# Splitting the first chunk's second-layer weights between the steps of the first projection, and taking weight tiles at the split

## The chip, the core and the metric

The kernel runs on one core of one Trainium2 chip. Its metric is the device time of one execution in microseconds (us). Five engines take part: TensorE (PE, with its weight loads shown apart as PEld), VectorE (DVE), ScalarE (ACT), GpSimd (POOL) and SyncE (SP), which here issues the DMAs.

## What is computed

A transformer block with adaptive layer norm, in fp32: S = 2048 rows, D = 576, H = 32 heads of 18, a hidden layer of 4608.

```python
mod = (silu(c) @ w_mod).reshape(1, 6, 1, 576)          # sa, ca, ga, sb, cb, gb
h = layernorm(x) * (1 + ca) + sa
x = x + ga * (softmax(q @ k.T * Dh**-0.5) @ v  @ wo)    # q, k, v = h @ wqkv, 32 heads
h = layernorm(x) * (1 + cb) + sb
x = x + gb * (silu(h @ w1) @ w2)
```

## The kernel before

**Blocks and slots.** The 2048 rows are taken as four blocks of 512. For each block the attention runs head quad by head quad (8 quads), and its inner work is cut into slots: per slot TensorE makes two score matmuls into `psa` (line 812; VectorE takes their maximum, `mx`, line 814) and two into `psb` (line 863; ScalarE takes their exponential into `pt`, line 865). The products with V go to `psv` (line 900). All the other matmul work of the preceding block is laid between the slots as "filler": the output projection (`psp`, function `proj`), the second layer norm, the transposes of its result (`psT`, `h_T`), and the two layers of the MLP (`ps1`, `mlp1`; `ps2`, `mlp2`).

**Who sets the order.** TensorE's order is written out by the code: a planner (`Plan`) keeps an estimated time `plan.t`, and at each turn a slot, a piece of PV or a piece of filler is put down. Data decides when an instruction may start, but TensorE never runs a later instruction ahead of an earlier one. The loop also calls `serve` once a turn, which puts down the handling of weights described next. VectorE, ScalarE, POOL and SP have each one queue in program order as the framework's scheduler has put it.

**Precision and weights.** Every matmul is done in fp32r with operands in a high and a low part, so a weight tile has two halves in its second dimension. In block 0 the weights come raw from the inputs: `load_half` issues a DMA of half a tile into one of three `raw` buffers; `split_half` makes the parts on POOL. A half of `wo` or of `w2` takes three POOL instructions (multiply by the gate `ga` or `gb`, line 701; cast to the high part, line 702; subtract for the low part, line 705), a half of `w1` two (lines 704 and 705). `split_half` is put down when its load is `LAND` planner-ns old; its first instruction waits for the last score matmul put down ahead of it (`after_pe`). After the second half, `store_one` writes the split tile to a scratch array, `STORE` planner-ns later. Blocks 1 to 3 read the split tiles from there. `settle` puts down whatever is missing when a matmul needs the tile.

**MLP in chunks.** 36 tiles of `w1` and of `w2` are used in chunks of four (`CH`): `mlp1` for four hidden tiles (in pairs), then `mlp2` for the four 128-row tiles j of the block. `w1` tiles live in a ring of four (`W1B`), `w2` tiles in a ring of five; `wo` uses the same two rings before them.

**The stage around the change**, in block 0: `o_T` splits the attention output into `th` and `tl`; then the projection runs for j = 0 to 3, 14 parts each. At its end `add_x1` adds it to the residual `x1`: one half of the columns on VectorE (line 1010), the other through ScalarE (`gt`, line 1013) and POOL (line 1014). The layer norm of tile j follows while the projection of tile j + 1 runs: statistics (`ln_stat`, line 1020, two instructions, the second needs POOL's half of the add; aggregate, line 1023), the power on POOL (`r`, line 388), four small VectorE instructions (`ln_rs`, lines 394 to 398), the normalised row (`ob`, line 402) and a 64-column copy on POOL (line 403). Then eight planner-us without filler (`LP`), five `h_T` (transposes on TensorE, `etmp` on ScalarE, cast `hh` on VectorE, line 409, `hl` on POOL, line 413; the last one with `h2`, line 1053, and 64 rows of `hh`, line 415, both on POOL), and the first `mlp1`. In between are the loads of `w1` tiles 0 to 3 and `w2` tiles 0 to 3; `w1` tiles 4 and 5 are asked for while the second `mlp1` runs.

## Time and profile before

| | us |
|---|---|
| three timed runs | 2376.93, 2377.96, 2383.35 |
| their median | 2377.96 |
| the profiled execution's own time | 2377.5 |
| its span, first to last instruction | 2375.7 |
| PE busy | 2306.1 |
| DVE busy | 1784.3 |
| ACT busy | 1479.9 |
| POOL busy | 714.1 |

The times named below count from the start of the span. The output projection of block 0 runs from 567 to 598 us, its five `h_T` from 608 to 616, its MLP from 616 to about 1146. The profile's pages show for each engine the busy time, for each group of instructions what ended the idle time before it, and in slices the clock that was granted to TensorE (1.00 is full, 0.50 half). Matmul ends are modelled, so that a matmul row that follows another closely says little about how full TensorE is; an idle gap with the name of an instruction that ended it says more.

### The profile page before, as it was taken

What the parts mean: (1) busy time and instruction counts of PE and PEld (TensorE: products, weight loads), DVE (VectorE), ACT (ScalarE), POOL (GpSimd) and SP (SyncE); (2) the same over time, 40 slices, a digit from 0 to 9 for tenths busy, and PEclk for the clock granted to TensorE, in tenths of its full rate; (3) what the DMA queues carried; (4) which work ended last, traced back from release to release, by engine and by line L of the source; (5) the groups of instructions that cost most, each with busy time, mean ns of one, the idle gap of its engine ahead of it and who ended that gap; (6) DMA issues with size and microseconds to landing.
All of it is one profiled execution on the core that took longest, in us unless ns stands there. A gap on an engine that the chain in (4) does not pass through costs nothing.

```text
span 2375.7 us, 52168 instructions
## 1 busy us (share of the span) xinstructions
PE 2306.1 (97%) x19844; PEld 1576.7 (66%) x19844; DVE 1784.3 (75%) x3089; ACT 1479.9 (62%) x2710; POOL 714.1 (30%) x873
## 2 busy tenths in 40 slices
PE   5999999998899999999999999999999999989999
PEld 4874444434467777766666766767676676678998
DVE  8768889887878888887888888887888887144333
ACT  5237777775667777775777777775777777722121
POOL 5113433315747676654211111122211111110000
PEclk9999999999999999999999999999999999999999
DMA  7455556454656666665654445554655554335663
GB/s 254 161 178 173 177 169 183 161 173 152 210 183 223 216 226 219 220 214 172 220 183 168 158 164 192 168 183 134 201 160 188 177 187 153 114 134 208 214 204 115
DMA packets 201475, 433.02 MB, mean 182 GB/s; under 512 B 31362, under 2 KB 67618, under 8 KB 201226
## 3 DMA queue, kind: packets, MB, share of 16 engines
q1 hardware_dynamic: 201226, 429.68, 54.9%
q8 instruction: 159, 2.61, 0.5%
q14 instruction: 90, 0.74, 0.1%
HBM read 338.54 MB, written 86.33 MB: 179 GB/s over the span
## 4 chain that ended last, share of the span: by engine, by line
PE 85%; DVE 6%; DMA 3%; POOL 2%; ACT 2%; issue 1%; SPq 0%; DVEq 0%; POOLq 0%; ACTq 0%
PE ps L486 25%; PE psv L900 18%; PE psa L812 14%; PE ps L480 10%; PE psb L863 8%; PE psqk L599 4%; DVE mx L814 2%; PE psv L486 2%; PE psp L486 1%; DMA raw<-in_w 1%; PE psqk L486 1%; PE psv L1361 1%; ACT pt L865 1%; PE psqk L1361 1%; PE psp L480 1%
## 5 line engine op out<-in xcount | busy, mean ns | idle before, releaser
L814 DVE TENSOR_REDUCE mx<-psa 128x1 f32<-128x512 f32 x2048 | 1329.9, 684 | 285.3 <-PE psb L863 153.6
L865 ACT ACTIVATE pt<-psb 128x512 f32<-128x512 f32 x2048 | 1143.0, 598 | 482.6 <-PE psb L863 294.0
L863 PE MATMUL psb<-qt,kb 56*128 56x512 f32 x2048 | 754.6, 422 | 7.9 <-ACT pt L865 7.4
L812 PE MATMUL psa<-ka,qt 54*128 54x512 f32 x2016 | 722.8, 416 | 9.2 <-DVE mx L814 8.0
L812 PEld LDWEIGHTS psa<-ka,qt 54*128 54x128 f32 x2016 | 339.7, 186 | 306.3 <-DVE mx L814 204.6
L900 PE MATMUL psv<-pt,vt 128*32 128x512 f32 x4096 | 512.0, 603 | 1.0 <-ACT ov L904 1.0
L486 PE MATMUL ps<-w2t,g 64*128 64x288 f32 x4992 | 408.6, 293 | 0.9 <-POOL w2t L705 0.6
L486 PEld LDWEIGHTS ps<-w2t,g 64*128 64x128 f32 x4992 | 382.8, 186 | 29.1 <-DVE mx L814 5.0
L863 PEld LDWEIGHTS psb<-qt,kb 56*128 56x128 f32 x2048 | 352.6, 185 | 48.5 <-ACT pt L865 32.9
L486 PE MATMUL ps<-hh,w1t 64*128 64x512 f32 x1944 | 359.9, 395 | 5.2 <-POOL w1t L704 1.8
L1136 POOL TENSOR_TENSOR g<-etmp,g 128x512 fp32r<-128x512 f32 x108 | 137.6, 1295 | 381.4 <-ACT g L1135 269.7
L900 PEld LDWEIGHTS psv<-pt,vt 128*32 128x32 f32 x4096 | 100.0, 109 | 211.6 <-issue 205.1
L486 PEld LDWEIGHTS ps<-hh,w1t 64*128 64x128 f32 x1944 | 197.8, 187 | 50.6 <-DVE mx L814 5.9
L1014 POOL TENSOR_TENSOR x<-x,gt 128x288 f32<-128x288 f32 x116 | 93.1, 803 | 424.6 <-ACT gt L1013 424.6
L486 PE MATMUL ps<-hl,w1t 64*128 64x512 f32 x864 | 180.9, 393 | 0.0
L1010 DVE TENSOR_TENSOR x<-ps,x 128x288 f32<-128x288 f32 x184 | 83.9, 456 | 127.0 <-PE ps L480 76.5
L480 PE MATMUL ps<-w2t,g 128*128 128x288 f32 x960 | 132.9, 299 | 7.4 <-ACT g L1135 5.9
L480 PEld LDWEIGHTS ps<-w2t,g 128*128 128x128 f32 x960 | 130.5, 191 | 9.9 <-ACT g L1135 6.3
L1132 ACT ACTIVATE eq<-ps 128x512 f32<-128x512 f32 x36 | 21.5, 598 | 146.4 <-PE ps L480 146.4
L480 PE MATMUL ps<-hh,w1t 128*128 128x512 f32 x360 | 106.9, 390 | 0.5 <-DVE hh L415 0.5
L486 PEld LDWEIGHTS ps<-hl,w1t 64*128 64x128 f32 x864 | 90.2, 187 | 15.3
L1133 DVE SCALAR_TENSOR_TENSOR etmp<-etmp 128x512 f32<-128x512 f32 x108 | 78.5, 765 | 23.6 <-ACT etmp L1132 22.9
(150 smaller groups left out, 2138.4 us busy)
## 6 DMA issues: line engine op xcount, KB each, us to landing
w1t<-w1s SPq DMA_DIRECT2D x108, 640.0 KB
w2t<-w2s SPq DMA_DIRECT2D x108, 576.0 KB
kb<-kscr SPq DMA_DIRECT2D x512, 108.0 KB
ka<-kscr SPq DMA_DIRECT2D x504, 108.0 KB
w1s<-w1t SPq DMA_DIRECT2D x36, 640.0 KB
w2s<-w2t SPq DMA_DIRECT2D x36, 576.0 KB
vt<-vscr SPq DMA_DIRECT2D x32, 608.0 KB
qt<-qscr SPq DMA_DIRECT2D x128, 108.0 KB
```

The costliest lines, as they stand in the source:

```text
L480: mm(self.ps[late], lhsT=lhsT, rhs=rhs, start=(i == 0), stop=(i == self.n - 1))
L486: done = mm(self.ps[g], lhsT=lhsT[rows], rhs=rhs[rows], start=(s == 0), stop=(s == self.end))
L599: mm(qk_ps[0], lhsT=w[b][:, kt, :], rhs=(hTl if a else hTh)[:, kt, n * 512:(n + 1) * 512], start=(i == 0), stop=(i == 13))
L812: mm(ps, lhsT=t["q"][64 * j:64 * j + 54, hp, stt * P:(stt + 1) * P], rhs=t["a" if ("a", kc, hp) in t else "b", kc, hp][64 * j:64 * j + 54, ...
L814: return lambda: nc.vector.tensor_reduce(t["mx"][:, 2 * j + hp, stt, kc:kc + 1], ps, axis=AX.X, op=ALU.max)
L863: state["pe"] = mm(ps, lhsT=t["b", kt // 4, hp][64 * e:64 * e + 56, kt % 4 * P:(kt % 4 + 1) * P], rhs=t["q"][64 * e:64 * e + 56, hp, :], s ...
L865: nc.scalar.activation(t["P"][kt, hp][:, e, :], ps, AF.Exp, scale=SCALE)
L900: mm(t["ps"][32 * h:32 * h + 32, :], lhsT=t["v"][:, c0:c0 + 32], rhs=t["P"][kt, h // 2][:, h % 2, :], start=(kt == 0), stop=(kt == NKT - 1 ...
L1010: nc.vector.tensor_add(c["x1"][j][:, hs], ps, c["x1"][j][:, hs])
L1014: nc.gpsimd.tensor_add(c["x1"][j][:, hs], c["x1"][j][:, hs], t)
L1133: nc.vector.scalar_tensor_tensor(t, t, 1.0, u, op0=ALU.add, op1=ALU.mult)
L1136: (nc.vector if last else nc.gpsimd).tensor_tensor(g[:, 1, :], t, f(g[:, 0, :]), op=ALU.subtract)
```

## The change

Four things change, all of them in block 0 but for the two numbers.

- `w2` tiles 0 to 3 are asked for at parts 1, 4, 7 and 10 of the first projection (j = 0), not after the last norm step. `w1` tiles 2 and 3 are asked for after the fourth and fifth `h_T`, tiles 4 and 5 at parts 9 and 11 of the first `mlp1`. For the last chunk the last three `w2` tiles are asked for near the end of the preceding `mlp2`.
- A flag `ln` keeps `serve` from putting down a split from the end of a tile's projection to that tile's `ln_rs`.
- A tile of the ring is taken when its first half is split (`make`), not when it is asked for; `hold` keeps the split back until the ring's old tile has been used, and a store of the old tile that is still due is put down first.
- `LAND` goes from 5000 to 6000 planner-ns, `STORE` from 4000 to 8000.

The instructions of TensorE, VectorE and ScalarE are the same ones in the same order as before. POOL has the same instructions in another order, and so has SP with its DMAs.

**Place 1.** POOL's queue behind the first projection of block 0. `x` is the residual of a tile (its number tells tiles apart), `r` the power of the norm, `ob` the normalised row. Before:

```order
L1014 TENSOR_TENSOR x_6608<-x_6608,gt 128x288
L388 TENSOR_TENSOR r_7272<-ve,mhalf 128x1
L403 COPY ob<-ob 128x64
L1014 TENSOR_TENSOR x_6610<-x_6610,gt 128x288
L388 TENSOR_TENSOR r_7385<-ve,mhalf 128x1
L403 COPY ob<-ob 128x64
```

Of the change (lines 707, 708 and 711 are 701, 702 and 705 of before, 1023 is 1014):

```order
L1023 TENSOR_TENSOR x_6603<-x_6603,gt 128x288
L388 TENSOR_TENSOR r_7278<-ve,mhalf 128x1
L403 COPY ob<-ob 128x64
L707 TENSOR_TENSOR raw<-raw,gb 128x288 x2
L708 CAST w2t<-raw 128x288 x2
L711 TENSOR_TENSOR w2t<-raw,w2t 128x288 x2
L1023 TENSOR_TENSOR x_6605<-x_6605,gt 128x288
L388 TENSOR_TENSOR r_7402<-ve,mhalf 128x1
```

Both halves of `w2` tile 0 now stand between the copy of the first tile's `ob` and the add of the second tile's `x`. The same six stand ahead of the third tile's add (for `w2` tile 1) and of the fourth's (tile 2); of tile 3 the first half stands around the fourth tile's `r`, the second behind its `ob`.

**Place 2.** POOL's queue at the five `h_T`. `hl`, `h` (that is `h2`) and `hh` are what the first `mlp1` reads. Before:

```order
L704 CAST w1t<-raw 128x320
L413 TENSOR_TENSOR hl<-etmp,hh 128x512
L705 TENSOR_TENSOR w1t<-raw,w1t 128x320
L413 TENSOR_TENSOR hl<-etmp,hh 128x512
L704 CAST w1t<-raw 128x320
L705 TENSOR_TENSOR w1t<-raw,w1t 128x320
L704 CAST w1t<-raw 128x320
L413 TENSOR_TENSOR hl<-etmp,hh 128x512
L701 TENSOR_TENSOR raw<-raw,gb 128x288
L705 TENSOR_TENSOR w1t<-raw,w1t 128x320
L1053 CAST h_7841<-etmp 128x512
L415 TENSOR_TENSOR hh<-etmp,hh 64x512
```

Of the change:

```order
L710 CAST w1t<-raw 128x320
L711 TENSOR_TENSOR w1t<-raw,w1t 128x320
L413 TENSOR_TENSOR hl<-etmp,hh 128x512 x4
L1063 CAST h_7864<-etmp 128x512
L415 TENSOR_TENSOR hh<-etmp,hh 64x512
L710 CAST w1t<-raw 128x320
L711 TENSOR_TENSOR w1t<-raw,w1t 128x320
```

No split stands any more between the `hl` and ahead of `h` and `hh`; those of `w1` tiles 2 and 3 follow them.

**Place 3.** POOL's queue ahead of `w1` tiles 4 and 5, which the third `mlp1` reads; `g` is the output of an `mlp1`. Before:

```order
L705 TENSOR_TENSOR w2t<-raw,w2t 128x288
L701 TENSOR_TENSOR raw<-raw,gb 128x288
L1136 TENSOR_TENSOR g<-etmp,g 128x512
L702 CAST w2t<-raw 128x288
L1136 TENSOR_TENSOR g<-etmp,g 128x512
L705 TENSOR_TENSOR w2t<-raw,w2t 128x288
L704 CAST w1t<-raw 128x320
L705 TENSOR_TENSOR w1t<-raw,w1t 128x320
L704 CAST w1t<-raw 128x320
L705 TENSOR_TENSOR w1t<-raw,w1t 128x320
L704 CAST w1t<-raw 128x320 x2
L705 TENSOR_TENSOR w1t<-raw,w1t 128x320 x2
```

Of the change:

```order
L710 CAST w1t<-raw 128x320
L711 TENSOR_TENSOR w1t<-raw,w1t 128x320
L710 CAST w1t<-raw 128x320
L1157 TENSOR_TENSOR g<-etmp,g 128x512
L711 TENSOR_TENSOR w1t<-raw,w1t 128x320
L1157 TENSOR_TENSOR g<-etmp,g 128x512
L710 CAST w1t<-raw 128x320
L711 TENSOR_TENSOR w1t<-raw,w1t 128x320
L710 CAST w1t<-raw 128x320
L711 TENSOR_TENSOR w1t<-raw,w1t 128x320
L710 CAST w1t<-raw 128x320
L711 TENSOR_TENSOR w1t<-raw,w1t 128x320
L1157 TENSOR_TENSOR g<-etmp,g 128x512 x2
```

Before, the halves of `w1` tiles 4 and 5 stood behind 24 instructions for `w2` tiles 0 to 3 and behind the first two `g`; now they stand around these two, and no `w2` is left ahead of them.

```diff
@@ -59,7 +59,7 @@
 LP = 8000
 PB = 9
 PVMAX, PVMIN = 5, 3
-EACH, LAND, STORE = (1500, 2000), 5000, 4000
+EACH, LAND, STORE = (1500, 2000), 6000, 8000
 QKB = 3
 GS = 2
 GR = [[range(i, min(i + GS, n)) for i in range(0, n, GS)] for n in (28, 27)]
@@ -632,7 +632,7 @@
         qk_store(which, m, n, hl, (1, 0))
 
 
-    state = {"now": 0, "pe": None, "p": 0, "b": 0, "tail": False, "tail2": False}
+    state = {"now": 0, "pe": None, "p": 0, "b": 0, "tail": False, "tail2": False, "ln": False}
     fill = Filler(plan)
     qk_w = {}
 
@@ -667,14 +667,15 @@
                         fill.add(200, lambda a=mt_: mod_piece(*a), mode="full")
 
     asks, flight, stores = [], [], []
+    RING = {"w1": W1B, "w2": 5}
     last_load = [0]
 
-    def weights(key, w, src, scr, first, gate=None):
+    def weights(key, make, n, src, scr, first, gate=None, hold=None):
 
         if not first:
-            nc.sync.dma_start(f(w), f(scr))
+            nc.sync.dma_start(f(make()), f(scr))
             return
-        ask = {"key": key, "w": w, "src": src, "scr": scr, "gate": gate, "n": w.shape[2] // 2, "at": 0, "halves": [0, 1]}
+        ask = {"key": key, "make": make, "src": src, "scr": scr, "gate": gate, "n": n // 2, "hold": hold, "halves": [0, 1]}
         i = len(asks)
         while key[0] == "w1" and i and asks[i - 1]["key"][0] == "w2" and len(asks[i - 1]["halves"]) == 2:
             i -= 1
@@ -694,6 +695,11 @@
     def split_half():
 
         _, ask, h, raw = flight.pop(0)
+        if h == 0:
+            tag = ask["key"][0] if ask["key"][0] != "wo" else None
+            while tag and any(it[3] == (tag, ask["key"][1] - RING[tag]) for it in stores):
+                store_one()
+            ask["w"] = ask["make"]()
         w, gate, n = ask["w"], ask["gate"], ask["n"]
         cs = slice(h * n, h * n + n)
         hi = w[:, 1, cs]
@@ -704,18 +710,18 @@
             after_pe(nc.gpsimd.tensor_copy(hi, raw))
         nc.gpsimd.tensor_tensor(w[:, 0, cs], raw, f(hi), op=ALU.subtract)
         if h:
-            stores.append((plan.t + STORE, w, ask["scr"]))
+            stores.append((plan.t + STORE, w, ask["scr"], ask["key"]))
 
     def store_one():
 
-        _, w, scr = stores.pop(0)
+        _, w, scr, _ = stores.pop(0)
         nc.sync.dma_start(f(scr), f(w))
 
     def serve():
 
         if stores and stores[0][0] <= plan.t:
             store_one()
-        if flight and flight[0][0] + LAND <= plan.t:
+        if flight and flight[0][0] + LAND <= plan.t and not state["ln"] and not (flight[0][1]["hold"] and flight[0][1]["hold"]()):
             split_half()
         if asks and len(flight) < 3 and last_load[0] + EACH[asks[0]["gate"] is not None] <= plan.t:
             load_half()
@@ -951,12 +957,14 @@
         pool = mp["p"]
         c = ready[b] = {}
         for kt in range(KT):
-            if kt < 4:
-                w = pool.tile([P, 2, KT * P], F32R, tag="w1", name="wo1", bufs=W1B)[:, :, :D]
-            else:
-                w = pool.tile([P, 2, D], F32R, tag="w2", name="wo2", bufs=5)
-            weights(("wo", kt), w, wo[:, kt, :], wos[kt], b == 0, ga)
-            c["wo", kt] = w
+            def make(kt=kt):
+                if kt < 4:
+                    c["wo", kt] = pool.tile([P, 2, KT * P], F32R, tag="w1", name="wo1", bufs=W1B)[:, :, :D]
+                else:
+                    c["wo", kt] = pool.tile([P, 2, D], F32R, tag="w2", name="wo2", bufs=5)
+                return c["wo", kt]
+
+            weights(("wo", kt), make, D, wo[:, kt, :], wos[kt], b == 0, ga)
         c["x1"] = []
         for j in range(NST):
             c["x1"].append(pool.tile([P, D], F32, name="x1", bufs=5))
@@ -1000,6 +1008,7 @@
             for s in GP[part]:
                 c["pp"].step(s)
             if part == len(GP) - 1:
+                state["ln"] = b == 0
                 for g in range(2):
                     add_x1(j, g, c["pp"].ps[g])
                     plan.op("AV"[g == 0], plan.t + 200, 440, c["pp"].release[g])
@@ -1026,6 +1035,7 @@
 
         def ln_rs(j):
             c["rs", j] = rstd_b(pool, *c["ve", j], 1)
+            state["ln"] = False
             plan.op("V", plan.t, 770)
 
         def ln_c(j):
@@ -1071,6 +1081,8 @@
             steps_ = dict(zip((1, 4, 8, 11), ln_steps(j - 1))) if j else {}
             for part in range(len(GP)):
                 fl.add(MMH * len(GP[part]), lambda j=j, part=part: proj(j, part), need={0: pair_need if j else o_need, len(GP) // 2: half_need}.get(part))
+                if b == 0 and j == 0 and part in (1, 4, 7, 10):
+                    fl.add(0, lambda i=part // 3: w2_load(i))
                 if part in steps_:
                     fl.add(0, steps_[part])
         for step in ln_steps(3):
@@ -1083,12 +1095,20 @@
             fl.add(LP)
 
         def w_load(i):
-            c["w1", i] = pool.tile([P, 2, KT * P], F32R, tag="w1", name="w1t", bufs=W1B)
-            weights(("w1", i), c["w1", i], w1[i], w1s[i], b == 0)
+            def make():
+                c["w1", i] = pool.tile([P, 2, KT * P], F32R, tag="w1", name="w1t", bufs=W1B)
+                return c["w1", i]
+
+            weights(("w1", i), make, KT * P, w1[i], w1s[i], b == 0, None, lambda: i >= c["room"])
 
         def w2_load(i):
-            c["w2", i] = pool.tile([P, 2, D], F32R, tag="w2", name="w2t", bufs=5)
-            weights(("w2", i), c["w2", i], w2[i], w2s[i], b == 0, gb)
+            def make():
+                c["w2", i] = pool.tile([P, 2, D], F32R, tag="w2", name="w2t", bufs=5)
+                return c["w2", i]
+
+            weights(("w2", i), make, D, w2[i], w2s[i], b == 0, gb, lambda: i > c["freed"] + 1)
+
+        c["freed"], c["room"] = CH - 1, W1B
 
         def etmp():
             if last:
@@ -1118,6 +1138,7 @@
                 c["p1"].step(s)
             if part < NG - 1:
                 return
+            c["room"] = i + 2 + W1B
             us = c["p1"].ps
             if not state["tail"]:
 
@@ -1148,6 +1169,8 @@
                 c["p2"].step(s)
             if part < len(G2) - 1:
                 return
+            if j == NST - 1:
+                c["freed"] = i0 + 2 * CH - 1
             for hf in range(2):
                 add_x1(j, hf, c["p2"].ps[hf])
                 plan.op("AV"[hf == 0], plan.t + 200, 440, c["p2"].release[hf])
@@ -1161,17 +1184,17 @@
         if not EARLY:
             for kt in range(KT):
                 fl.add(440, lambda kt=kt: h_T(kt), name=["h_T"], need=hT_need, mode="full")
-        for i in range(4):
+        for i in range(4 if b else 2):
             fl.add(0, lambda i=i: w_load(i))
-        fl.add(0, lambda: w2_load(0))
-        if b == 0:
-            for i in range(1, 4):
-                fl.add(0, lambda i=i: w2_load(i))
+        if b:
+            fl.add(0, lambda: w2_load(0))
         if EARLY:
             if b == 0:
                 fl.add(LP)
             for kt in range(KT):
                 fl.add(440, lambda kt=kt: h_T(kt), name=["h_T"], need=hT_need, mode="full")
+                if b == 0 and kt > 2:
+                    fl.add(0, lambda i=kt - 1: w_load(i))
 
         def w_at(n, *loads):
 
@@ -1191,17 +1214,19 @@
                     add(MMH * len(G2[part]), lambda j=j, part=part: mlp2(i0, j, part), None, {0: pair_need, len(G2) // 2: half_need}.get(part))
                     w_at(j * len(G2) + part, *loads)
 
-        add_mlp1(0)
+        add_mlp1(0, *([] if b else [(9, w_load, 4), (11, w_load, 5)]))
         for i0 in range(0, NFT, CH):
             if i0 + CH < NFT:
                 w2s_ = [(0, w2_load, i0 + 1), (4, w2_load, i0 + 2), (9, w2_load, i0 + 3)] if i0 or b else []
-                if i0 == 0:
+                if i0 == 0 and b:
                     w2s_ += [(1, w_load, 4), (3, w_load, 5)]
                 add_mlp1(i0 + 2, *w2s_)
                 add_mlp1(i0 + CH, (6, w_load, i0 + 6), (11, w_load, i0 + 7))
-                add_mlp2(i0, fl.add, (2, w_load, i0 + 8), (9, w_load, i0 + 9), (18, w2_load, i0 + 4))
+                final = b == 0 and i0 + 2 * CH == NFT
+                add_mlp2(i0, fl.add, (2, w_load, i0 + 8), (9, w_load, i0 + 9), (18, w2_load, i0 + 4),
+                         *([(22, w2_load, i0 + 5), (23, w2_load, i0 + 6), (24, w2_load, i0 + 7)] if final else []))
             else:
-                add_mlp1(i0 + 2, (0, w2_load, i0 + 1), (2, w2_load, i0 + 2), (4, w2_load, i0 + 3))
+                add_mlp1(i0 + 2, *([(0, w2_load, i0 + 1), (2, w2_load, i0 + 2), (4, w2_load, i0 + 3)] if b else []))
         if last:
             add_mlp2(NFT - CH, fl.add)
         else:
```

## The prediction

> **What bounds the kernel now.** I read the page first, then the waits by engine, then the clock in short windows, then the rows of block 0's projection.
>
> ```profile
> PE 2306.1 (97%) x19844; PEld 1576.7 (66%) x19844; DVE 1784.3 (75%) x3089; ACT 1479.9 (62%) x2710; POOL 714.1 (30%) x873
> ```
>
> TensorE is at work for 97% of the span, and by the order its list of matmuls does not change. So a microsecond is won only where TensorE stands still or runs at a lower clock, and lost only where it is made to stand still. Its own waits, from the view of waits for this engine (total, times, longest):
>
> ```profile
> PE psa L812 <- DVE mx L814: 8.0, 12, 1.8
> PE ps L486 <- POOL w1t L704: 1.8, 1, 1.8
> PE ps L486 <- POOL w1t L705: 1.7, 1, 1.7
> PE ps L486 <- POOL hh L415: 1.6, 1, 1.6
> PE ps L486 <- POOL w2t L705: 0.6, 2, 0.5
> ```
>
> The four rows with POOL are what this change can take away: 1.8 + 1.7 + 1.6 + 0.6. The first row is what it can make worse. The timeline of TensorE says where they lie (start, length, and in brackets the idle time and what ended it):
>
> ```profile
> 593.53 0.50 PE L812 MATMUL psa<-ka,qt 54*128 54x512 f32 x1 [1.79 <-DVE mx L814]
> ...
> 619.55 0.49 PE L812 MATMUL psa<-ka,qt 54*128 54x512 f32 x1 [0.58 <-DVE mx L814]
> ...
> 624.00 0.49 PE L486 MATMUL ps<-hh,w1t 64*128 64x512 f32 x1 [1.62 <-POOL hh L415]
> ...
> 650.49 0.51 PE L486 MATMUL ps<-hh,w1t 64*128 64x512 f32 x2 [1.82 <-POOL w1t L704]
> 652.68 0.61 PE L486 MATMUL ps<-hh,w1t 64*128 64x512 f32 x1 [1.69 <-POOL w1t L705]
> ```
>
> All lie within 60 us of block 0. The same stretch in windows of 3.4 us (length, TensorE busy, granted clock, DMA share, GB/s):
>
> ```profile
> 591.50:594.90 3.40, 1.61 (x20) 1.00 0.14 50
> 594.90:598.30 3.40, 3.40 (x26) 0.50 0.01 2
> 618.80:622.20 3.40, 2.82 (x23) 1.00 0.83 282
> 622.20:625.60 3.40, 1.78 (x14) 1.00 0.64 239
> 625.60:629.00 3.40, 3.40 (x18) 0.50 0.42 135
> 649.50:652.90 3.40, 0.72 (x4) 1.00 0.82 267
> 652.90:656.30 3.40, 3.40 (x18) 0.50 0.74 301
> ```
>
> A window in which TensorE is busy for 1.78 us or less is followed by one at half the clock; the one with 2.82 is not. A full window at half the clock does 1.7 us of work in 3.4, so each wait of that size costs 1.7 us more than it shows.
>
> **The change part by part.** The sum is made against the profiled execution's 2377.5 us (its span and 1.8 around it), which is 0.5 below the median of the runs. The instructions are the same, so nothing is added or removed by count; only waits change.
>
> *Ahead of the first `mlp1` (place 2).* The wait at 622.4 is for the last `hh`, which POOL did late:
>
> ```profile
> 617.87 1.02 DVE L409 CAST hh<-etmp 128x512 fp32r<-128x512 f32 x1
> ...
> 622.00 0.61 POOL L1053 CAST h<-etmp 128x512 fp32r<-128x512 f32 x1
> 622.69 1.26 POOL L415 TENSOR_TENSOR hh<-etmp,hh 64x512 fp32r<-64x512 f32 x1
> ```
>
> VectorE's cast for it was done at 618.9. Without splits in between, POOL has after that at most the last `hl` (1.3 us, an estimate from the 1.26 of the like instruction beside it) and then 0.61 + 1.26: 618.9 + 3.2 = 622.1, where TensorE arrives at 622.4. I take all of the 1.62. The 0.58 of VectorE at 619 comes in the same jam, in which that cast took 1.02; I take it as gone too. Bounds for the two: 1.0 to 2.2.
>
> *The third `mlp1` (place 3).* Behind `hh`, POOL had 23 instructions for `w2` ahead of the halves of `w1` tiles 4 and 5; now it has eight for `w1` tiles 2 and 3. From the view of one tile (`raw`: least, median and longest ns, first and last start):
>
> ```profile
> L704 POOL CAST w1t<-raw x72: 439/451/913, 602.1 to 1044.4; 128x320 fp32r<-128x320 f32 x72
> L705 POOL TENSOR_TENSOR w1t<-raw,w1t x72: 857/873/1182, 602.6 to 1045.6; 128x320 fp32r<-128x320 f32 x72
> L701 POOL TENSOR_TENSOR raw<-raw,gb x72: 784/807/1267, 620.4 to 1087.7; 128x288 f32<-128x288 f32 x72
> L702 POOL CAST w2t<-raw x72: 414/423/782, 624.0 to 1089.2; 128x288 fp32r<-128x288 f32 x72
> L705 POOL TENSOR_TENSOR w2t<-raw,w2t x72: 791/807/1356, 624.5 to 1091.6; 128x288 fp32r<-128x288 f32 x72
> ```
>
> Some eight halves of 0.81 + 0.42 + 0.81 = 2.0 us, 16 us, leave the place, and four of 0.45 + 0.87 = 1.3, 5.3 us, come. That is 10 us of room for a wait of 3.5, so 1.82 + 1.69 = 3.5 go; if the later load of these tiles eats the room, 0. Late next is the pair of `psa` and `mx`, with VectorE 25% idle; I leave 0 for it.
>
> *The half clock.* With these waits gone, the windows from 625.6 and 652.9 run at full clock: 2 x 1.7 = 3.4.
>
> The Trainium skill bears on this: "TensorE: Matmul & The Clock Gate", Part 1, What's actually happening, has the clock halved after at least one idle window of about 3.4 us. By that rule waits of 1.6 to 1.8 us would cost no clock, and the sum below would lose its 3.4 and end at 2375.6. The trace disagrees: the window from 622.2 was busy for 1.78 us and the next was at 0.50. I go by the trace, and keep the other as a rival.
>
> *Later chunks.* The 0.6 for `w2t` at 985 and 1038 are waits for the second tile of a chunk. Its halves are no longer behind each other's; I take 0.6, bounds 0 and 0.6. `LAND` and `STORE` move splits and stores by 1 and 4 planner-us; POOL's 30% hides them. A store that comes later holds SP's queue, and with it the next `ka` and `kb`, only if its split isn't done, which 8 us cover.
>
> *Behind the projection (place 1): the cost.* POOL's rows there before:
>
> ```profile
> 580.81 0.24 POOL L403 COPY ob<-ob 128x64 f32<-128x64 f32 x1 [1.57 <-DVE ob L402]
> 581.96 0.80 POOL L1014 TENSOR_TENSOR x<-x,gt 128x288 f32<-128x288 f32 x1 [0.92 <-ACT gt L1013]
> ...
> 586.88 0.24 POOL L403 COPY ob<-ob 128x64 f32<-128x64 f32 x1 [1.45 <-DVE ob L402]
> 587.91 0.80 POOL L1014 TENSOR_TENSOR x<-x,gt 128x288 f32<-128x288 f32 x1 [0.79 <-ACT gt L1013]
> ```
>
> Only 0.9 us lie between a copy of `ob` and the next add of `x`, and two halves of a `w2` tile now stand there. Their length, from nine such instructions of `wo`:
>
> ```profile
> 535.15 2.31 POOL L701 TENSOR_TENSOR raw<-raw,ga 128x288 f32<-128x288 f32 x3 [12.72 <-DMA x<-in_x]
> 537.40 1.16 POOL L702 CAST wo<-raw 128x288 fp32r<-128x288 f32 x3
> 538.53 2.31 POOL L705 TENSOR_TENSOR wo<-raw,wo 128x288 fp32r<-128x288 f32 x3
> ```
>
> Three halves took 535.15 to 540.84, 5.7 us, so two take 3.8. From 581.05 they end at 584.85, the add at 585.65. Who waits for it stands in VectorE's queue:
>
> ```profile
> 582.72 1.27 DVE L814 TENSOR_REDUCE mx<-psa 128x1 f32<-128x512 f32 x2
> 583.90 0.45 DVE L1020 BATCH_NORM_STATS2 st<-x 128x6 f32<-128x288 f32 x1
> ...
> 586.73 1.28 DVE L814 TENSOR_REDUCE mx<-psa 128x1 f32<-128x512 f32 x2
> ...
> 589.97 0.45 DVE L1020 BATCH_NORM_STATS2 st<-x 128x6 f32<-128x288 f32 x1
> ```
>
> The second statistics can start at 585.7, not 583.9: VectorE stands for 1.8 us, and the two `mx` behind it, at 586.73, go to 588.5. TensorE has three `psa` banks, and no slack there:
>
> ```profile
> 587.12 0.84 PE L812 MATMUL psa<-ka,qt 54*128 54x512 f32 x2
> ```
>
> The second of these two needs the bank of the `mx` that begins at 586.73, and could only start when that ended, 0.3 us behind the first. So TensorE is 1.8 late. The flag `ln` keeps a split out of the norm steps, yet not from the place ahead of the add that feeds them. The third tile has the same build-up (copy 586.88, add 587.91, statistics 589.97): 1.8 more, together 3.6. For the fourth tile there is room:
>
> ```profile
> 598.05 0.80 POOL L1014 TENSOR_TENSOR x<-x,gt 128x288 f32<-128x288 f32 x1 [4.88 <-ACT gt L1013]
> ```
>
> POOL idled for 4.9 us ahead of its add, and 3.8 fit: 0. Bounds: 0, if VectorE were ahead of TensorE, to 11.5 (below).
>
> The pause at 593.5 grows from 1.8 to 3.6 and keeps its half-clock window. The new one of 1.8 near 587.5 lies in one 3.4-us window about half the time: 0.5 x 1.7 = 0.85.
>
> **The sum.** 2377.5 + 3.6 + 0.85 - 1.62 - 0.58 - 3.5 - 3.4 - 0.6 = 2372.2 us, 5.3 us or 0.22% less. Behind it nothing gives the time back or takes it: TensorE bounds the rest, and DMAs wait for matmuls, not for the clock on the wall.
>
> **Rivals.**
>
> *The projection does not pay.* If VectorE can reach the `mx` before TensorE needs the bank, 3.6 and 0.85 fall away: 2367.8. For it: VectorE is idle 25% of the span. Against it: TensorE's pause before 593.53 is already a wait for VectorE.
>
> *The half clock stays*, put there by something else in those windows: 2372.2 + 3.4 = 2375.6. Against it stand the three pairs of windows above; for it, that the rows show which window follows which, not the cause.
>
> *The splits hold the norm longer than they win*: slower. One mechanism, the add of the next tile queued behind two halves, at the price of a half at its longest, or with its raw tile not yet landed:
>
> ```profile
> 559.85 0.79 POOL L701 TENSOR_TENSOR raw<-raw,ga 128x288 f32<-128x288 f32 x1 [2.39 <-DMA raw<-in_wo]
> ```
>
> At the maxima of the three `w2` rows above a half takes 1.27 + 0.78 + 1.36 = 3.4 us; two take 6.8. Then the second and third tiles lose 4.8 each and the fourth 6.8 - 4.9 = 1.9, 11.5 in all; with two more half-clock windows the sum is 2377.5 + 11.5 + 3.4 - 9.7 = 2382.7. It turns slower when two halves take over 6.4 us (2 x (6.4 - 2.0) + 0.85 = 9.7). A wait of 2.4 us for a landing, as at 559.85, does the same.
>
> *It does not do what it says*: 2377.5. Against it stands the order itself.
>
> **How the numbers follow.** Forecast 0.54 (2372.2, its own range 2369.5 to 2375); no price in the projection 0.18 (2367.8); half clock stays 0.14 (2375.6); slower 0.10 (2382.7); no effect 0.04. From 2366.5 to 2379.5 lie the forecast, most of the second, and the third and fifth. A measurement of this kernel can tell about 0.3% from no change, 7.1 us: faster than that are nearly all of the second case and a quarter of the first, 0.30; slower are some of the fourth, 0.06; the rest 0.64.
>
> **What would show it.** In the profile after: no wait of TensorE for `hh` near 622 and none for `w1t` in block 0; full clock in the two windows behind them; VectorE idle for about 1.8 us ahead of the second statistics of the second and third tiles, with POOL's add of `x` ending its wait; the pause of TensorE near 593 at about 3.6 us in place of 1.8. I am wrong if VectorE does not stand there, if the clock still halves near 625 and 653, or if a wait for a raw tile or a store appears at SP or POOL.

## The result and the profile after

The changed kernel takes 2386.71 us (median of nine runs, 2382.84 to 2392.65), the kernel before 2379.21 us (nine runs, 2376.93 to 2384.27): 1.0029 times as long, with a 95% interval of 1.0019 to 1.0039. By these medians it is slower by 7.5 us, where 5.3 us less were forecast, and outside the range.

The profiled execution of the change is its longest run (span 2390.8 us, 15.1 more than the profile of before). Some 7 us of these lie ahead of block 0's projection, where no request was moved (last section). So the two profiles are compared by stages. TensorE's list of matmuls is the same in all kernels here, and the start of the same matmul in the list ends a stage in each of them. Stage 1 goes from 12 us ahead of block 0's projection into its `h_T` (555.2 to 615.4 us in the kernel before), stage 2 into the first chunk's `mlp2` (674.0), stage 3 over the later chunks (1058.9), stage 4 to the last matmul (2371.9):

| us | 1 | 2 | 3 | 4 | 1 to 4 |
|---|---|---|---|---|---|
| before | 60.2 | 58.6 | 385.0 | 1313.0 | 1816.7 |
| the change | 65.2 | 49.0 | 397.1 | 1313.3 | 1824.6 |
| difference | +5.0 | -9.6 | +12.1 | +0.3 | +7.9 |

Stages 1 and 2 are what the prediction spoke of most: its terms there were 3.6 + 0.85 = +4.45, and -(1.62 + 0.58 + 3.5 + 3.4) = -9.1. In this pair of profiles the whole surprise is stage 3; the runs below show a second one in stage 1, which in the profile of before happens to be long. By the profile's page TensorE is as busy as before, and no engine's sum tells of it:

```profile
PE 2312.6 (97%) x19844; PEld 1580.0 (66%) x19844; DVE 1780.7 (74%) x3089; ACT 1481.9 (62%) x2710; POOL 712.2 (30%) x873
```

In the waits of TensorE of the changed kernel (total, times, longest), those for `hh` and `w1t` of before are gone and two rows are new or grown:

```profile
PE psa L818 <- DVE mx L820: 12.2, 14, 3.5
PE ps L486 <- POOL w2t L711: 5.8, 6, 1.2
PE ps L486 <- POOL w2t L708: 3.9, 3, 2.5
```

Nine waits for `w2t`, 9.7 us, stand where before had two of 0.6. The first row grew from 8.0 to 12.2. Over stage 3 TensorE stands still for 10.5 us in place of 2.2, and 6.8 us run at half clock in place of none, which costs 3.4: together 11.7 of the 12.1. The timeline of TensorE shows the two waits of the first kind in the projection and the worst pair of the second:

```profile
596.44 0.50 PE L818 MATMUL psa<-ka,qt 54*128 54x512 f32 x1 [1.71 <-DVE mx L820]
...
604.23 0.79 PE L818 MATMUL psa<-ka,qt 54*128 54x512 f32 x1 [3.52 <-DVE mx L820]
...
995.82 0.61 PE L486 MATMUL ps<-w2t,g 64*128 64x288 f32 x2 [2.47 <-POOL w2t L708]
997.39 0.85 PE L486 MATMUL ps<-w2t,g 64*128 64x288 f32 x3 [0.96 <-POOL w2t L711]
```

**Stage 1.** VectorE's and POOL's rows of the second and third tile show the mechanism of the forecast: POOL's add of `x` (line 1023) starts behind two halves, and VectorE's second statistics (1029) wait for it.

```profile
588.03 0.24 POOL L403 COPY ob<-ob 128x64 f32<-128x64 f32 x1 [1.56 <-DVE ob L402]
588.22 1.58 POOL L707 TENSOR_TENSOR raw<-raw,gb 128x288 f32<-128x288 f32 x2
589.74 0.80 POOL L708 CAST w2t<-raw 128x288 fp32r<-128x288 f32 x2
590.50 1.57 POOL L711 TENSOR_TENSOR w2t<-raw,w2t 128x288 fp32r<-128x288 f32 x2
592.03 0.80 POOL L1023 TENSOR_TENSOR x<-x,gt 128x288 f32<-128x288 f32 x1
```

```profile
592.87 0.46 DVE L1029 BATCH_NORM_STATS2 st<-x 128x6 f32<-128x288 f32 x1 [1.66 <-POOL x L1023]
...
600.67 0.46 DVE L1029 BATCH_NORM_STATS2 st<-x 128x6 f32<-128x288 f32 x1 [1.64 <-POOL x L1023]
```

**Stage 3.** This is POOL's queue of the change at the pair of waits above:

```profile
992.56 0.80 POOL L707 TENSOR_TENSOR raw<-raw,gb 128x288 f32<-128x288 f32 x1
994.94 0.45 POOL L710 CAST w1t<-raw 128x320 fp32r<-128x320 f32 x1 [1.58 <-DMA raw<-in_w]
995.34 0.43 POOL L708 CAST w2t<-raw 128x288 fp32r<-128x288 f32 x1
995.73 0.86 POOL L711 TENSOR_TENSOR w1t<-raw,w1t 128x320 fp32r<-128x320 f32 x1
996.55 0.79 POOL L711 TENSOR_TENSOR w2t<-raw,w2t 128x288 fp32r<-128x288 f32 x1
```

The reader is to see the second row. The last half of the chunk's `w2` is multiplied by the gate at 992.56, and then the first cast of the next `w1` tile stands in the middle of it and waits for a raw half that has not landed. TensorE, which needs the `w2` half now, waits for a DMA that it does not need. The kernel before has the same half in one piece:

```profile
982.59 1.25 POOL L701 TENSOR_TENSOR raw<-raw,gb 128x288 f32<-128x288 f32 x1
983.90 0.42 POOL L702 CAST w2t<-raw 128x288 fp32r<-128x288 f32 x1
984.41 0.80 POOL L705 TENSOR_TENSOR w2t<-raw,w2t 128x288 fp32r<-128x288 f32 x1
985.76 0.45 POOL L704 CAST w1t<-raw 128x320 fp32r<-128x320 f32 x1 [0.55 <-issue]
```

The change has such a `w1` cast inside an open half of `w2` at six places of block 0, and the kernel before at none.

The clock, in windows of 3.4 us laid on its grid (length, TensorE, its weight loads, VectorE, ScalarE, POOL busy, granted clock, DMA share, GB/s):

```profile
592.90:596.30 3.40, 1.83 (x27) 1.50 (x24) 2.52 (x9) 1.57 (x4) 1.01 (x3) 1.00 0.82 257
596.30:599.70 3.40, 3.26 (x34) 2.10 (x36) 2.70 (x6) 1.05 (x2) 3.40 (x6) 1.00 0.02 9
599.70:603.10 3.40, 1.01 (x14) 0.68 (x11) 1.55 (x8) 1.23 (x3) 1.49 (x3) 1.00 0.84 221
603.10:606.60 3.50, 2.37 (x16) 2.28 (x18) 2.87 (x5) 0.60 (x1) 1.56 (x4) 0.51 0.58 196
...
654.40:657.80 3.40, 3.40 (x29) 1.86 (x22) 3.13 (x7) 3.16 (x7) 1.16 (x2) 1.00 0.77 261
...
992.30:995.70 3.40, 1.05 (x15) 0.81 (x13) 0.83 (x2) 1.27 (x3) 1.82 (x4) 1.00 0.62 194
995.70:999.10 3.40, 2.32 (x12) 2.00 (x14) 0.40 (x1) 0.37 (x1) 3.40 (x5) 0.50 0.32 75
```

The two half-clock windows behind the `hh` and `w1t` waits are gone (654.4 runs at 1.00). Behind the 3.52 us pause stand two (603.1 to 609.9), where one stood behind the 1.79 of before, and two new ones follow the pair of waits near 995.

### The profile page after: what moved, and what is told of

Same layout as the page of the kernel before. It is cut to its first block, busy times and chain, and to the rows that moved or that the text cites. A ratio compares the mean times of both kernels' runs of the same rounds, so it can differ in the third digit from the quotient of the medians.

```text
span 2390.8 us, 52181 instructions
## 1 busy us (share of the span) xinstructions
PE 2312.6 (97%) x19844; PEld 1580.0 (66%) x19844; DVE 1780.7 (74%) x3089; ACT 1481.9 (62%) x2710; POOL 712.2 (30%) x873
## 4 chain that ended last, share of the span: by engine, by line
PE 83%; DVE 5%; DMA 5%; POOL 3%; ACT 2%; issue 1%; SPq 0%; POOLq 0%; ACTq 0%; DVEq 0%
PE ps L486 24%; PE psv L906 17%; PE psa L818 13%; PE ps L480 10%; PE psb L869 8%; PE psqk L599 4%; DVE mx L820 2%; PE psv L486 2%; DMA raw<-in_w 1%; PE psp L486 1%; PE psv L1386 1%; PE psqk L1386 1%; PE psqk L486 1%; DMA qt<-qscr 1%; PE psp L480 1%
## 5 line engine op out<-in xcount | busy, mean ns | idle before, releaser
L818 PE MATMUL psa<-ka,qt 54*128 54x512 f32 x2016 | 725.0, 417 | 13.6 <-DVE mx L820 12.2
```

What stands on the lines that cost most here:

```text
L818: mm(ps, lhsT=t["q"][64 * j:64 * j + 54, hp, stt * P:(stt + 1) * P], rhs=t["a" if ("a", kc, hp) in t else "b", kc, hp][64 * j:64 * j + 54, ...
```

## The experiments

First theory, A: the age `LAND` of 6000 planner-ns is at fault, because each of three raw buffers is held longer and the loads wait for buffers. SP's waits with a raw load in front speak for it (change, then before):

```profile
SPq L689 <- POOL w2t L711: 50.4, 27, 5.7
```

```profile
SPq L688 <- POOL w2t L705: 32.6, 15, 4.5
```

Rivals: B, taking tiles at the split with its holds; C, the later store.

**Age back to 5000** (in the change):

```diff
-EACH, LAND, STORE = (1500, 2000), 6000, 8000
+EACH, LAND, STORE = (1500, 2000), 5000, 8000
```

> The change with LAND back at 5000; all else is the change, STORE 8000 included. Theory A (the age limit): with three raw buffers and an age of 6000 planner-ns a half is split and its buffer given back later, the loads behind it wait, and the last halves of a chunk's w2 come too late for the second layer; then the nine waits of TensorE for w2t (9.7 us in the profile of the change) shrink to the 0.6 of before or less, and about 10 to 12 us go from the time of the change: 0.998 to 0.9995 of before. Theory B (taking the tile at the split, with its hold and the stores put ahead) makes the halves late: nothing goes, 1.003. Theory C (the later store): 1.003.

**Age 6000 alone** (in the kernel before):

```diff
-EACH, LAND, STORE = (1500, 2000), 5000, 4000
+EACH, LAND, STORE = (1500, 2000), 6000, 4000
```

> The kernel before with LAND at 6000 and nothing else. Theory A: waits for w2t of 5 to 12 us with their half-clock windows appear in the later chunks, 1.002 to 1.005 of before. Theories B and C: 1.000, and the waits for w2t stay at 0.6.

**Store back to 4000** (in the change):

```diff
-EACH, LAND, STORE = (1500, 2000), 6000, 8000
+EACH, LAND, STORE = (1500, 2000), 6000, 4000
```

> The change with STORE back at 4000, LAND at 6000. Theory C (a later store holds SP's queue, and with it the next load): the waits for w2t go, 0.998 to 0.9995 of before. Theories A and B: they stay near 9.7 us, 1.003.

| | ratio to before, 95% | 1 | 2 | 3 | TensorE waits for `w2t` |
|---|---|---|---|---|---|
| before | 1 | 60.2 | 58.6 | 385.0 | 0.6 |
| the change | 1.0029 (1.0019 to 1.0039) | 65.2 | 49.0 | 397.1 | 9.7 |
| change, age 5000 | 0.9993 (0.9983 to 1.0003) | 68.7 | 48.2 | 384.2 | 0.2 |
| before, age 6000 | 1.0071 (1.0056 to 1.0085) | 58.2 | 64.8 | 397.4 | 9.3 |
| change, store 4000 | 1.0020 (1.0010 to 1.0031) | 64.8 | 49.7 | 396.0 | 9.2 |

The age is at fault for stage 3: one number gives it back in the change (397.1 to 384.2), and the same number alone puts 12.4 us into it in the kernel before. Theory C, the store, is out. But with the age of before the change is still only 1.7 us faster by the ratio, with an interval that reaches 1: stage 2 won 10.4 us and stage 1 lost 8.5. Beyond the pauses of the change, TensorE stood there a third time, for the fourth tile, and ran at half clock from 616.6 to 626.8:

```profile
614.86 0.50 PE L818 MATMUL psa<-ka,qt 54*128 54x512 f32 x1 [2.23 <-DVE mx L820]
```

POOL's rows have three halves of `w2` (from 604.09) ahead of the fourth tile's add of `x` (610.47); in the change two stand there. With age 6000 the old order of requests is hit in stage 2 too; three waits for `w1t` there came to 11.1 us:

```profile
PE ps L486 <- POOL w1t L704: 6.7, 2, 3.7
...
PE ps L486 <- POOL w1t L705: 4.4, 1, 4.4
```

**Only the taking at the split** (kernel before with `make`, `hold`, the stores put ahead and the flag `ln`; requests and numbers as before). The edit is those lines of the diff shown with the change, without the moved requests.

> The kernel before with only the taking of tiles at the split (with hold, the stores put ahead and the flag ln); every request stands where it stood, LAND 5000, STORE 4000. Theory A: this part costs nothing and wins nothing, 0.9985 to 1.0015, waits for hh, w1t and w2t as before. Theory B: it delays w2, waits for w2t of some us, 1.002 or more.

Measured 0.9999 (0.9989 to 1.0008); stages 58.1, 58.5, 383.8; waits for `hh` 1.6, `w1t` 3.3, `w2t` 0.2. With the age of before it costs and wins nothing; theory B is out.

**No `w2` in the projection** (in the change, age 6000, then with age 5000):

```diff
-                if b == 0 and j == 0 and part in (1, 4, 7, 10):
-                    fl.add(0, lambda i=part // 3: w2_load(i))
...
-        add_mlp1(0, *([] if b else [(9, w_load, 4), (11, w_load, 5)]))
+        add_mlp1(0, *([] if b else [(9, w_load, 4), (11, w_load, 5)] + [(11, w2_load, i) for i in range(4)]))
```

> The change without w2 in the first projection: w2 tiles 0 to 3 are asked for at part 11 of the first mlp1, behind w1 tiles 4 and 5; LAND 6000, STORE 8000. If POOL's splits ahead of the adds of x cost what the profile of the change shows (TensorE 5 us later from 580 to 628 us), these 5 us go and the gains at hh and w1t stay: about 1.001 of before, with the waits for w2t of the later chunks as they are. Rival: the first chunk's w2 is now late, TensorE waits 4 us or more for w2t near 670, and nothing is won: 1.003.

> The run without w2 in the projection, now with LAND at 5000. By theory A the waits for w2t in the later chunks go, and the wait of 7.0 us at 662 for the first chunk's w2 shrinks, since its eight halves turn over in less time: 0.995 to 0.998 of before. Rival: the first w2 tile is late because it is asked for late, whatever the age; the wait near 662 stays above 5 us with half clock behind it: 0.999 or more.

Measured 1.0045 (1.0032 to 1.0057) with stages 56.0, 60.5, 400.7, and 0.9986 (0.9974 to 0.9998) with 57.9, 58.3, 383.4. Stage 1 is 7 to 9 us shorter than in the change, so the splits there do cost that much; but in stage 2 the rival of the first run came true, and the second lies between its two forecasts. The first chunk's `w2` is late, with age 6000:

```profile
669.33 2.71 PE L486 MATMUL ps<-w2t,g 64*128 64x288 f32 x6 [6.97 <-POOL w2t L708]
```

With 5000 this is 0.9 and 4.4 us.

**All splits held until the fourth norm** (in the change, age 5000):

```diff
-            if part == len(GP) - 1:
+            if part == 0 and j == 0:
                 state["ln"] = b == 0
+            if part == len(GP) - 1:
...
-            state["ln"] = False
+            state["ln"] = b == 0 and j < 3
```

> The change with LAND at 5000 and with no split from the first part of the first projection to the small norm instructions of the fourth tile; the loads of w2 stay where the change has them. If the splits ahead of the adds of x are the whole cost of the projection, the 8.5 us that the LAND-5000 run had lost by 628 us go, its gains at hh and w1t stay: 0.994 to 0.997 of before. Rival: the splits now pile up in the pause behind the norm and at the h_T, and hh, w1t or w2t are late again: 0.998 or more.

Measured 0.9983 (0.9972 to 0.9994), which is in the rival's range; stages 59.8, 56.2, 384.8. Stage 1 fell by 8.9 against the same kernel without the hold (68.7), as expected; a part of the rival holds as well, since in stage 2 waits are back at `hl` (1.27 us) and `hh` (2.07).

**One `w2` tile in the pause behind the norm** (in the kernel without `w2` in the projection), age 5000: tile 0 asked for behind `w1` tiles 0 and 1, tile 1 at part 0 of the first `mlp1`, 2 and 3 at part 11.

```diff
-        if b:
-            fl.add(0, lambda: w2_load(0))
+        fl.add(0, lambda: w2_load(0))
...
-        add_mlp1(0, *([] if b else [(9, w_load, 4), (11, w_load, 5)] + [(11, w2_load, i) for i in range(4)]))
+        add_mlp1(0, *([] if b else [(9, w_load, 4), (11, w_load, 5)] + [(0, w2_load, 1), (11, w2_load, 2), (11, w2_load, 3)]))
```

> As the run without w2 in the projection with LAND at 5000, but w2 tile 0 is asked for behind w1 tiles 0 and 1 and so split in the pause behind the norm, tile 1 at the start of the first mlp1, tiles 2 and 3 at its part 11. No split stands ahead of an add of x, eight instructions less wait behind w1 tiles 4 and 5: no wait for hh, w1t or w2t above 1 us, 0.993 to 0.996 of before. Rival: tile 0's splits hold up the hl and hh at the h_T, a wait of 1.5 us or more near 622 is back: 0.997 or more.

Measured 0.9959 (0.9944 to 0.9973): 2369.71 us against 2381.34, faster than both kernels. Stages 57.6, 50.2, 385.6: the gain of the change in stage 2 without its price in 1 and 3. Three rows for `hh` and `w2t` are left in TensorE's waits:

```profile
PE ps L486 <- POOL hh L415: 0.9, 1, 0.9
PE ps L486 <- POOL w2t L708: 0.6, 1, 0.6
...
PE ps L486 <- POOL w2t L711: 0.5, 1, 0.5
```

**Is it the buffers?** Four raw buffers in the change, age 6000 (the norm statistics of the MLP block go from three buffers to two for the space):

```diff
-        raw = mp["p"].tile([P, 320], F32, tag="raw", name="raw", bufs=3)[:, :n]
+        raw = mp["p"].tile([P, 320], F32, tag="raw", name="raw", bufs=4)[:, :n]
...
-        if asks and len(flight) < 3 and last_load[0] + EACH[asks[0]["gate"] is not None] <= plan.t:
+        if asks and len(flight) < 4 and last_load[0] + EACH[asks[0]["gate"] is not None] <= plan.t:
```

> The change with four raw buffers in place of three, and up to four halves in flight; LAND stays at 6000 (the norm statistics of the MLP block get two buffers in place of three to make room). Theory A1 (buffer turnover): the age of 6000 hurts because each of three buffers is held for it, so that loads wait for buffers; with four the waits for w2t fall from 9.7 us to under 1.5 and 8 to 12 us go from the time of the change, 0.998 to 1.000 of before. Theory A2 (the age by itself: the split is put down later in the program however many buffers there are): the waits stay above 6 us, 1.002 to 1.004.

Measured 1.0018 (1.0008 to 1.0027): between the two. SP's row fell from 50.4 to 11.8 us, but TensorE's waits for `w2t` only from 9.7 to 4.4, and stage 3 to 392.7. Theory A explains a part.

```profile
SPq L689 <- POOL w2t L711: 11.8, 5, 5.4
```

**A shorter age.** If a longer age is late, a shorter one should be early:

> The kernel with one w2 tile in the pause, with LAND at 4000 in place of 5000. Theory A (the later the split, the later the buffer and the half): the two waits for w2t that are left near 977 (1.0 us in all) go, 0 to 3 us less than with 5000, 0.993 to 0.996 of before. Rival: a split that is put down before its raw half has landed blocks POOL, with it g and hl; waits of POOL for raw grow from the first chunk on, and it is slower than with 5000: 0.997 or more.

> The kernel before with LAND at 4000 and nothing else. Theory A: the waits for w1t (3.5 us) and for w2t (0.6) shrink, with a half-clock window: 0.997 to 0.999. Rival as for the run beside it: POOL waits for landings, hh and w1t come no earlier, 1.000 to 1.003.

The edits are `LAND` 4000 in the kernel with one tile in the pause, and in the kernel before. Measured 1.0039 (1.0026 to 1.0052) and 1.0035 (1.0021 to 1.0048): stage 3 is 403.4 and 400.6, the waits for `w2t` 10.7 and 9.4. Theory A as first put, the later the worse, falls; with 4000 stage 3 loses as much as with 6000. The rival's sign is weak: from 560 to 1125 us POOL waited 95.4 us for raw halves of the weights against 92.2 with 5000, and in the kernel before 93.3 against 82.1. In SP's queue the stores now wait for their splits (52.8 us for `w2t` from 690 to 1125 us, 28.3 with 5000), which led to theory D: stores ahead of loads hold them.

**Later stores** (`STORE` 14000, with four buffers, with age 4000, and in the best kernel):

> The change with four raw buffers and LAND 6000, and STORE at 14000 in place of 8000. With four buffers SP's loads no longer waited for buffers (11.8 us in place of 50.4), but its stores waited 48.0 us for splits, and 4.4 us of waits for w2t were left. Theory D (a store that stands in SP's queue ahead of its split holds the loads behind it): with the later store SP's waits for splits fall by half or more, the waits for w2t to under 1.5 us, 0.997 to 1.000 of before. Theory A2 (the age by itself): the waits for w2t stay above 3.5 us, 1.001 to 1.003.

> The kernel with one w2 tile in the pause and LAND 4000, with STORE at 14000 in place of 8000. Theory D: the stores' waits in SP's queue (52.8 us for w2t there) fall by half or more and the 10.7 us of TensorE's waits for w2t to under 3: 0.994 to 0.998 of before. Rival (an earlier load lands late, whatever the stores): they stay above 7 us, 1.002 to 1.005.

> The kernel with one w2 tile in the pause, LAND 5000, with STORE at 14000 in place of 8000. Theory D: no more than the 1.0 us of waits for w2t near 977 to win, 0.994 to 0.9965. Rival: the tile of the ring is needed while its store is still due, so that the store is put ahead of the split and SP waits there: 0.997 or more.

Measured 1.0023 (1.0012 to 1.0035), 1.0030 (1.0017 to 1.0043) and 0.9955 (0.9941 to 0.9969); waits for `w2t` 5.3, 8.3 and 1.7. SP's stores still waited 48.3 and 49.2 us for `w2t` splits in the first two, in the same stretch. Theory D falls: a store put down later waits in another place for as long.

**Halves kept whole.** The order of POOL gave theory E, the `w1` cast inside a half of `w2`. It stands at six places in each of the six kernels so far with age 6000 (the two with four buffers too), at none to two places with 5000 and at none with 4000. The edit makes the first instruction of a split (`head`) follow the last of the split before:

```diff
-        nc.gpsimd.tensor_tensor(w[:, 0, cs], raw, f(hi), op=ALU.subtract)
...
+        if last_split[0] is not None:
+            tc.add_manual_dep(head.ins, last_split[0].ins.name, BEHIND, reason="halves stay whole")
+        last_split[0] = nc.gpsimd.tensor_tensor(w[:, 0, cs], raw, f(hi), op=ALU.subtract)
```

> The change as it is, LAND 6000 and three buffers, but each split starts only behind the last instruction of the split before it, so that POOL's queue keeps the three instructions of a half together. In the change the first cast of a w1 half stands inside a half of w2 (between its multiply and its cast) at six places in block 0, and there it waits 1 to 3 us for its raw half to land; before and in the kernels that are not late there is none. Theory E: this is what the age of 6000 costs; the nine waits for w2t (9.7 us) fall to 1 to 4 us, the half-clock windows behind them go, 0.998 to 1.001 of before. Theory A2 (the age by itself): they stay above 6 us, 1.002 to 1.004.

> The kernel before with LAND 6000 and the halves kept whole in the same way. Theory E: the waits for w2t (9.3 us with LAND 6000 alone) fall to 1 to 4 us, those for w1t in the first chunk (11.1 us) stay, since no half of w2 is opened there; 1.002 to 1.005 of before in place of 1.0071. Theory A2: no change, 1.006 to 1.008.

> The change with LAND 6000, halves kept whole and four raw buffers. Whole halves alone left 4.5 us of waits for w2t, four buffers alone 4.4. If the two causes (a w1 cast inside a w2 half; loads that wait for one of three buffers) are all that the age of 6000 brings, the waits for w2t fall under 1.2 us and the time from 674 to 1059 us of the kernel before is within 2 us of it: 0.997 to 1.0005. If the age by itself remains, 2 us or more of waits stay: 1.0005 to 1.002.

| age 6000 | ratio to before, 95% | stage 3 | waits for `w2t` |
|---|---|---|---|
| the change | 1.0029 (1.0019 to 1.0039) | 397.1 | 9.7 |
| + whole halves | 1.0006 (0.9996 to 1.0017) | 389.4 | 4.5 |
| + four buffers | 1.0018 (1.0008 to 1.0027) | 392.7 | 4.4 |
| + both | 1.0012 (1.0002 to 1.0022) | 388.4 | 2.5 |
| before, age 6000 | 1.0071 (1.0056 to 1.0085) | 397.4 | 9.3 |
| + whole halves | 1.0031 (1.0019 to 1.0042) | 388.3 | 4.4 |

Of the 12.1 us that stage 3 lost, whole halves give back 7.7, four buffers 4.4, both 8.7. The waits for `w2t` stayed above what was expected in all three runs with whole halves (1 to 4 us twice, under 1.2 with both), and in the kernel before those for `w1t` fell too, from 11.1 to 6.9 us. The totals give back less than stage 3 does, since in the change stage 1 is longer with whole halves in both profiles: 69.7 against 65.2 us, and 71.1 against 64.8 with four buffers. Whether the edit does that or chance is not shown. In the change with whole halves POOL goes through the same place without a stop:

```profile
983.19 0.79 POOL L708 TENSOR_TENSOR raw<-raw,gb 128x288 f32<-128x288 f32 x1
984.05 0.42 POOL L709 CAST w2t<-raw 128x288 fp32r<-128x288 f32 x1
984.55 0.79 POOL L715 TENSOR_TENSOR w2t<-raw,w2t 128x288 fp32r<-128x288 f32 x1
985.28 0.45 POOL L711 CAST w1t<-raw 128x320 fp32r<-128x320 f32 x1
```

```profile
984.52 0.40 PE L487 MATMUL ps<-w2t,g 64*128 64x288 f32 x2 [1.38 <-POOL w2t L709]
985.40 0.53 PE L487 MATMUL ps<-w2t,g 64*128 64x288 f32 x3 [0.48 <-POOL w2t L715]
```

Theory E is shown as the larger part of the cost of the age. The edit takes out more than the six casts: in the change a `w2` half also begins inside another `w2` half at 13 places (in the kernel before at nine). In the change these 13 waited for landings for 0.7 us in all (in the kernel before the nine for 4.3) and the six casts for 10.4, which speaks for the casts; no run took the two apart. At the place above 1.9 us are left of the 3.4, where the kernel before had 0.5. What keeps 2.5 us of waits with both edits was not taken apart either: the age itself is what remains, argued and not shown. Open too is why 4000 is late. In one place of the kernel with one tile in the pause and age 4000, the rows of SP show the last `w2` load behind a `qt` load that waited 4.8 us for `mscr` to land:

```profile
866.71 0.38 SPq L846 DMA_DIRECT2D mscr<-mt  x1
871.98 1.38 SPq L850 DMA_DIRECT2D qt<-mscr  x2
873.46 0.37 SPq L689 DMA_DIRECT2D raw<-in_w  x1
```

POOL then had nothing to split until 877.49, and TensorE stood for 3.33 us. That is one place; no run moved it.

## Why the prediction was wrong, step by step

- **The wait for `hh`, 1.62, all of it gone: right.** No matmul of block 0 waits for `hh` in the change. The 0.58 of VectorE at 619 did not go: pauses of 0.43 and 0.59 for `mx` end at 626.08 and 631.05.
- **The waits for `w1t`, 3.5: right.** With the two half-clock windows stage 2 won 9.6 where 9.1 was forecast. The kernel with age 6000 and the old order shows what the moved requests are worth when the halves come late: 11.1 us of waits in stage 2 that the change, with the same age, does not have.
- **The half clock, 3.4: right.** No half-clock window lies between 615 and 990 us in the change. By the rule of the Trainium skill ("TensorE: Matmul & The Clock Gate", Part 1, What's actually happening) an idle window comes first; here as before a window busy for 1.05 us of 3.4 (from 992.3) was enough, so the runs do not bear that rule out as it stands.
- **The price in the projection, 3.6 + 0.85: the mechanism right, the size too small.** VectorE waited 1.66 and 1.64 us for the add, with 1.8 forecast for each; TensorE's pauses there were 1.71 and 3.52, with 1.8 and 3.6 forecast. The stage lost 5.0 with 4.45 forecast, but that is in part luck: 60.2 is the longest stage 1 of the twelve profiles without splits ahead of these adds (56.0 to 60.2, mean 58.3). Against their mean the change lost 6.9, and the seven profiles with such splits (64.8 to 71.1, mean 67.4) lost 9.1. Two terms were too small. For the half clock half a window was put; stage 1 has three to eight half-clock windows in the seven profiles and none to two in the twelve. For the fourth tile 0 was put; the change bears it out (a pause of 0.25), but in five of the six other profiles with such splits TensorE paused there for 1.60 to 4.12 us, and in four of these POOL's rows have three halves, not two, ahead of that add. So the change with the age of before ended at 0.9993: even without the loss of stage 3 the 5.3 us were not reached.
- **"`LAND` and `STORE` move splits and stores by 1 and 4 planner-us; POOL's 30% hides them": this step failed, and it is the one that made the change slower.** It put 0, with 0.6 to win, on stage 3, which lost 12.1. `STORE` was free as far as the runs tell (1.0020 with 4000, 1.0029 with 8000, intervals that overlap). `LAND` was not, for two reasons that POOL's mean of 30% says nothing about. The split of a chunk's last half had no room: the rows that the prediction itself counted as 0.6 to be won, waits of 0.5 and 0.2 at 985 and 1038, said that these halves already came just too late (it took them for a chunk's second tile; in POOL's rows they are the second half of its last, the 28th and 32nd tile), and a step that moves them back by 1 us cannot be free there. And the scheduler laid the next tile's cast into the open half (why it does so with 6000 and not with 5000 is not shown); that stood in the order of POOL, which was quoted at three places, none of them in stage 3.
- **The rivals.** The one on the slower side (splits that hold the norm) needed halves of 3.2 us or more; two took 3.8 us in all, so it was not that. What made the change slower came from a place that no rival named.

## What to carry to other kernels

A delay that is costed at nothing needs the room of the tightest consumer, not the mean load of the engine: a wait of 0.5 us in the trace before says that this room is zero. On an engine that takes its queue in order look in the built order for an instruction that waits for a DMA standing inside another chain whose end somebody needs; an order-only dependency removes it. And when one change carries a mechanism and two retuned numbers, take the numbers apart first: here the requests moved out of the way of `hh` and `w1t` were worth 9.6 us in stage 2, one number cost 12.1 in stage 3, and the place where `w2` was split instead, ahead of the adds of `x`, cost 7 to 9 in stage 1. One pair of profiles read that price as 5.0; the stage over many profiles says more.

## What the runs showed that was not expected

The same instructions can take different times, by where the clock's windows fall. In the change's profile the 162.8 us window, in a stage that the change does not touch, ran at half the clock, as did the next, behind one that was busy for 1.90 us:

```profile
159.40:162.80 3.40, 1.90 (x7) 1.08 (x8) 2.09 (x4) 0.84 (x3) 0.15 (x2) 1.00 0.30 92
162.80:166.20 3.40, 3.40 (x9) 2.49 (x10) 1.31 (x2) 2.25 (x5) 0.00 (x0) 0.50 0.91 300
```

In the kernel before, the same pause was split between two windows and neither was followed by half clock:

```profile
154.60:158.00 3.40, 2.42 (x12) 1.23 (x8) 2.58 (x4) 0.82 (x3) 0.00 (x0) 1.00 0.30 92
158.00:161.40 3.40, 2.85 (x12) 1.73 (x12) 1.29 (x2) 2.94 (x6) 0.15 (x2) 1.00 0.71 219
161.40:164.80 3.40, 3.40 (x26) 1.01 (x26) 2.95 (x5) 2.61 (x5) 0.00 (x0) 1.00 0.77 299
```

The Trainium skill ("TensorE: Matmul & The Clock Gate", Part 1, What's actually happening) calls the window free-running and its phase different from run to run; these rows agree. Ahead of stage 1 TensorE ran at half clock for 20.4 us in the change's profile and for 3.4 in that of before; half of the difference is 8.5 us, about the 7.2 by which stage 1 starts later. In the 19 profiles it starts between 554.7 and 562.4 us. So a single profile carries several us of chance, and only the comparison by stages showed the 12 us of stage 3 clearly. There is also no sharp bound in the busy time as recorded: 1.83 us (from 592.9) was followed by full clock, 1.90 by half, and in the profile with four buffers and the later store even a window busy for 3.13 us (from 556.3) was.
